# A fused attention and MLP block on one core: the query copy of the last units moved to ScalarE, the gate steps moved to another slot, and the drain reordered

## The chip, the cores and the metric

The kernel runs on one core of a Trainium2 chip. The metric is the device time of one execution in microseconds (us). Three runs of the kernel before gave 1291.65, 1294.03 and 1294.50 us, so the median is 1294.03 us. The engines have the profile's names: PE is TensorE, PEld its weight loads, DVE is VectorE, ACT is ScalarE, POOL is GpSimd and SP is SyncE, which here only issues DMAs.

## What is computed

The reference, cut to what matters (2048 tokens, width 512, 32 heads of 128, 2048 cached keys per head):

```python
xn = layernorm(x)
q  = (xn @ wq) split into 32 heads of 128
p  = softmax(q @ k_cache^T * 128 ** -0.5)
s  = concat over heads (p @ v_cache) @ wo
h  = gelu(layernorm(xn) @ w1), its four column groups shifted by +1, -1, +2, -2 tokens
x1 = xn + h @ w2
g  = silu(x1 + gelu(layernorm(x1) @ w3) @ w4)
out = x + s * g
```

The MLP side ends in g, called the gate here. The kernel carries twice the gate, which explains the factor 0.5 that stands in front of it below.

## The kernel before

**Units and slots.** The attention is cut into 128 units, one for each head and block of 512 queries, in eight groups of four heads; inside a group the four query blocks follow each other, and inside a block the four heads. A unit has eight slots, p = 0 to 7, and each slot handles 256 keys. All engines' instructions are pinned: each engine runs them in the order in which the program issues them. The loop over slots (L656 to L713) is therefore the schedule.

**One slot.** PE multiplies two 128-key blocks by the queries into one of two PSUM tiles `ps_s` (`s_slot`, L178). ACT takes the exponential of the whole 128x1024 tile into `pT` (L188). Five slots later PE multiplies those weights with the values into `ps_o` (`pv_slot`, L207; the lag is `LAG = 5`).

**One unit on DVE.** The eight `pT` quarters are added up to one 128x512 tile: `add_first` at slot 4 (L194), `add_next` at slot 6 (L199), and at slot 0 of the following unit `add_last`, which is a third add and two folds (L199, L204, L205). At slot 3 of the following unit PE sums that tile over its partitions with four 128x1 matmuls against a column of ones (`sums`, L217), DVE takes the reciprocal (L227), SP writes it to DRAM (`dr`, L229) and at slot 4 reads it back broadcast to all partitions (`rb`, L244). At slot 2 of the unit after that, `norm` (L255) multiplies `ps_o` by `rb` into `oT`.

**Queries.** `q_mm` puts the next unit's queries into the PSUM tile `ps_q` with two matmuls in slot 0 and two in slot 1. `q_copy` (L173 to L176) brings them to the bf16 tile `qT` at slot 2; before the change DVE does it (L175). `ps_q` shares a single PSUM buffer (tag "xa") with `ps_wo`.

**Output projection.** When the four heads of a query block are done, its four blocks of 128 tokens get their product with Wo, one in each of the following units: two matmuls at slot 4, two at slot 5 (`wo_mm`, L260), and `wo_post` (L316) at slot 6 adds the result into the f32 sum `s_acc` (L322). In the last group `wo_post` also applies the gate and adds x (L326, L328) and stores the 128 tokens (L329). For query blocks 2 and 3 the projection of the group before the last is deferred: its normalized heads are kept in `oS`, and the last group's projection of these tokens has eight matmuls instead of four. So units 125, 126 and 127 have four more matmuls at slot 4 than others.

**Last units.** `QUIET` is 121 (units count from 0), and the MLP's matmuls are all done by then. `tail_open` loads the gate `gf` and the input `xf` of the last four token blocks. `gate_sum` (L290), called once in each of the units 122 to 125 at slot 7 (L653), turns `s_acc` of one of these token blocks into 0.5 * s_acc * gate + x with two DVE steps (L293, L295), so that only the deferred part remains to be added in the end.

**Drain.** After the loop (L715 to L749) the last unit, 127, still owes PE the value products of slots 3 to 7, all of its denominator sums (`split_sums`, L231, which feeds `ps_sum` with several partly added tiles, four 128x1 matmuls for each), one projection left over for token block 11 (`t11`), and the projection of token blocks 12 to 15, for which two PSUM tiles `pa` and `pb` hold two blocks each. `last_scale` (L297) multiplies by the gate on DVE (L299), `last_out` (L302) adds `s_acc` on POOL for two blocks and on DVE for two (L304), and SP stores them (L305). Slot 6 of unit 127 has a fold of its own on DVE in place of an add (L698). The drain's order of work is written out by hand.

Of the kernel before, what the change touches and what calls it, by code (L numbers as in the profile page):

```python
# [8 lines left out]
ACT = mybir.ActivationFunctionType  # L9
# [8 lines left out]
def kernel(  # L18
# [15 lines left out]
    nc = tc.nc  # L34
# [94 lines left out]
    def at(n, fn):  # L129
        todo[n].append(fn)  # L130
# [41 lines left out]

    def q_copy(u):  # L173
        qT = qtp.tile([P, 512], BF16, name="qT")
        pin(nc.vector.tensor_copy(out=qT[:], in_=st[u].pop("psq")[:]))  # L175
        st[u]["qT"] = qT  # L176

    def s_slot(u, p):  # L178
# [12 lines left out]
    def add_first(u):  # L191
        s = st[u]
        s["acc"] = trp.tile([P, 4, 512], BF16, name="acc")
        pin(nc.vector.tensor_tensor(  # L194
            out=s["acc"][:], in0=s["pT"][0][:], in1=s["pT"][1][:], op=ALU.add))
# [11 lines left out]
    def pv_slot(u, p):  # L207
        g, qt, hh = units[u]
        s = st[u]
        if p == 0:  # L210
            s["o"] = psO.tile([P, 512], FP32, name="ps_o")
        pT = s["pT"][p // 2]
        for j in range(2):
            kc = 2 * p + j
            mm(s["o"][:], vBs[g * HG + hh][:, kc, :], pT[:, 2 * (p % 2) + j, :], kc == 0, kc == KC - 1)
# [15 lines left out]
    def split_sums(u, parts):  # L231
        s = st[u]
        if "ps" not in s:
            s["ps"] = psX.tile([P, 4], FP32, tag="xm", name="ps_sum")
        for a, first, last in parts:
            a = a.rearrange("k (p j) -> k j p", j=4)
            for j in range(4):
                mm(s["ps"][:, j:j + 1], a[:, j, :], ones_t[:], first and j == 0, last and j == 3)
        if parts[-1][2]:
            recip(s, s["ps"])  # L240

    def bcast(u):
        st[u]["rb"] = rp.tile([P, 512], FP32, name="rb")
        pin(nc.sync.dma_start(  # L244
            out=st[u]["rb"][:], in_=st[u]["dr"][:].rearrange("p j -> (p j)").partition_broadcast(P)))

    def norm(u, pieces=1):
        g, qt, hh = units[u]
        s = st.pop(u)
        if hh == 0:  # L250
            oTs[(g, qt)] = otp.tile([P, HG, 512], BF16, name="oT")
        w = 512 // pieces
        for i in range(pieces):
            c = slice(i * w, (i + 1) * w)
            pin(nc.vector.tensor_tensor(  # L255
                out=oTs[(g, qt)][:, hh, c], in0=s["o"][:, c], in1=s["rb"][:, c], op=ALU.mult))
# [3 lines left out]
    def wo_mm(g, t, hhs):  # L260
        if hhs[0] == 0:
            wo_box[0] = psX.tile([P, D], FP32, tag="xa", name="ps_wo")
        held = g == NG - 1 and (NG - 2, t // 4) in deferred
        if held and hhs[0] == 0:
            wo_part(wo_box[0][:], g - 1, t, range(HG), True, False)
        wo_part(wo_box[0][:], g, t, hhs, hhs[0] == 0 and not held, hhs[-1] == HG - 1)

    def wo_part(ps, g, t, hhs, first, last):
        oT = oTs[(g, t // 4)]
        ts = t % 4  # L270
        for hh in hhs:
            mm(ps, oT[:, hh, ts * P:(ts + 1) * P], wos[g * HG + hh][:],
               first and hh == hhs[0], last and hh == hhs[-1])
# [16 lines left out]
    def gate_sum(t):  # L290
        gf, xf = tl[t]
        sa = s_acc[:, t, :]
        pin(nc.vector.scalar_tensor_tensor(  # L293
            out=sa, in0=sa, scalar=0.5, in1=gf[:], op0=ALU.mult, op1=ALU.mult))
        pin(nc.vector.tensor_tensor(out=sa, in0=sa, in1=xf[:], op=ALU.add))  # L295
# [6 lines left out]
    def last_out(t, eng):  # L302
        gf, xf = tl.pop(t)
        pin(eng.tensor_tensor(out=xf[:], in0=gf[:], in1=s_acc[:, t, :], op=ALU.add))  # L304
        pin(nc.sync.dma_start(out=out2d[t * P:(t + 1) * P, :], in_=xf[:]))  # L305
# [10 lines left out]
    def wo_post(g, t):  # L316
        ps = wo_box.pop(0)
        sa = s_acc[:, t, :]
        if g == 0:
            pin(nc.vector.tensor_copy(out=sa, in_=ps[:]))  # L320
            return
        pin(nc.vector.tensor_tensor(out=sa, in0=ps[:], in1=sa, op=ALU.add))  # L322
        if g < NG - 1:
            return
        xl, gl = fin.pop(t)
        pin(nc.vector.scalar_tensor_tensor(  # L326
            out=gl[:], in0=sa, scalar=0.5, in1=gl[:], op0=ALU.mult, op1=ALU.mult))
        pin(nc.vector.tensor_tensor(out=xl[:], in0=gl[:], in1=xl[:], op=ALU.add))  # L328
        pin(nc.sync.dma_start(out=out2d[t * P:(t + 1) * P, :], in_=xl[:]))  # L329
# [320 lines left out]

    at(QUIET * SPU, tail_open)
    for t in range(4 * LQ, NT):
        at((QUIET + 1 + t % 4) * SPU + 7, lambda t=t: gate_sum(t))  # L653

    wo_todo = deque()
    for n in range(NS):  # L656
        u, p = divmod(n, SPU)
        s_slot(u, p)
        m = n - LAG
        if m >= 0:  # L660
            pv_slot(*divmod(m, SPU))
        if u == 0 and p in (0, 2, 4):
            q_mm(1 + p // 2, range(DC))
        if u == 0 and p in (1, 3, 5):
            q_copy(1 + p // 2)
        if p in (0, 1) and HG - 1 <= u < NU - 1:
            q_mm(u + 1, (2 * p, 2 * p + 1))
        if p == 0 and u >= 1:
            add_last(u - 1)
        if p == 2 and HG - 1 <= u < NU - 1:  # L670
            q_copy(u + 1)
        if p == 2 and u >= 2:
            norm(u - 2)
            gg, qq, hh = units[u - 2]
            if hh == HG - 1 and (gg, qq) in deferred:
                pin(nc.sync.dma_start(out=o_d[qq][:], in_=oTs[(gg, qq)][:]))
            elif hh == HG - 1:
                wo_todo.extend((gg, 4 * qq + ts) for ts in range(4))
                if gg == NG - 1:
                    fin_load(4 * qq)  # L680
        if p == 3 and u >= 1:
            sums(u - 1)
        if p == 4 and u >= 1:
            bcast(u - 1)
        if p in (4, 5) and wo_todo:
            wo_mm(*wo_todo[0], (0, 1) if p == 4 else (2, 3))
        if p == 6 and wo_todo:
            gg, t = wo_todo.popleft()
            wo_post(gg, t)
            if gg == NG - 1 and t % 4 < 3:  # L690
                fin_load(t + 1)
        if p == 4:
            add_first(u)
        if p == 6 and u < NU - 1:
            add_next(u, 2)
        if p == 6 and u == NU - 1:
            a = st[u]["acc"]
            pin(nc.vector.tensor_tensor(out=a[:, 0:2, :], in0=a[:, 0:2, :], in1=a[:, 2:4, :], op=ALU.add))  # L698
        if p in (2, 3, 6, 7):
            w = 2 * u + (p >= 4)  # L700
            i = p % 2
            if i == 0:
                want = -(-(w + 1 - W0) * NCH // (W1 - W0)) if w >= W0 else 0
                window.pop("run", None)
                if done < min(want, NCH):
                    if done in hooks:
                        hooks.pop(done)(n)
                    window["run"] = chunks.popleft()
                    done += 1
            if "run" in window:  # L710
                window["run"](i, n)
        for fn in todo.pop(n, ()):
            fn()  # L713
# [4 lines left out]
    gg, t11 = wo_todo.popleft()  # L718
    ts = [4 * LQ + j for j in range(4)]
    norm(U - 1)  # L720
    pv_slot(U, 3)
    wo_mm(gg, t11, (0, 1))
    pv_slot(U, 4)
    wo_mm(gg, t11, (2, 3))
    wo_post(gg, t11)
    pv_slot(U, 5)
    pa = psS.tile([P, 2, 512], FP32, name="ps_s")
    wo_part(pa[:, 0, :], GL - 1, ts[0], range(HG), True, False)
    split_sums(U, [(s["acc"][:, i, :], i == 0, False) for i in range(2)]
               + [(s["pT"][2][:, i, :], False, False) for i in range(4)]  # L730
               + [(s["pT"][3][:, i, :], False, False) for i in range(2)])
    pv_slot(U, 6)
    split_sums(U, [(s["pT"][3][:, i, :], False, i == 3) for i in range(2, 4)])
    bcast(U)
    pv_slot(U, 7)
    wo_part(pa[:, 1, :], GL - 1, ts[1], range(HG), True, False)
    pb = psS.tile([P, 2, 512], FP32, name="ps_s")
    for j in (2, 3):
        wo_part(pb[:, j % 2, :], GL - 1, ts[j], range(HG), True, False)
    dst = [(pa, pa, pb, pb)[j][:, j % 2, :] for j in range(4)]  # L740
    for j in range(4):
        wo_part(dst[j], GL, ts[j], range(HG - 1), False, False)
    norm(U, 2)
    for j in range(4):
        wo_part(dst[j], GL, ts[j], (HG - 1,), False, True)
        last_scale(ts[j], dst[j])
    for j in range(4):
        last_out(ts[j], nc.gpsimd if j < 2 else nc.vector)
    ph.close()  # L749


# [28 lines left out]
```

## Time and profile before

| What | us |
|---|---|
| median of three runs | 1294.03 (1291.65 to 1294.50) |
| profiled execution, its own time | 1291.04 |
| its span, first to last instruction | 1289.3 |
| PE busy | 1257.6 (98%) |
| ACT busy | 1111.7 (86%) |
| DVE busy | 1017.9 (79%) |
| POOL busy | 145.8 (11%) |
| granted TensorE clock, mean | 0.998 |
| unit 121, from its `sums` to the next unit's | 8.76 |
| units 123 and 124, the same | 9.66 each |
| from the end of the loop's matmuls (1269.70) to the end of the span | 19.60 |

The page's busy time of PE counts the modelled length of pipelined matmuls; a 128x512 matmul shows about 0.38 us by itself, while in a dense stretch one starts every 0.216 us. Where the text speaks of PE time it uses these starts. "Start to start" on DVE and ACT means the distance between the starts of two instructions that follow each other without a wait; they overlap a little (a lone exponential takes 1.02 us, three in a run take 2.86 us).

### The profile page before, as it was taken

To read this page: it belongs to the slowest core of one execution; us is meant where nothing else is said; L and a number is where in the kernel's file an instruction comes from. 1 tells how busy PE (TensorE), PEld (TensorE's weight loads), DVE (VectorE), ACT (ScalarE), POOL (GpSimd) and SP (SyncE) were. 2 spreads that over 40 slices of the span, in tenths; PEclk is the share of its full clock that TensorE was granted. 3 is DMA by queue.
4 is the path that set the end of the run, shared out by engine and by line. 5 is a ranking of instruction groups with operands and counts; after the bars stand their busy time and mean duration, and the time that the engine had idled before them with its cause. 6 is when DMAs were issued, how large, how long until landed. Compare 5 with 4: busy or idle time off the path is not lost.

```text
span 1289.3 us, 17150 instructions
## 1 busy us (share of the span) xinstructions
PE 1257.6 (98%) x6148; PEld 577.4 (45%) x6272; DVE 1017.9 (79%) x1396; ACT 1111.7 (86%) x1189; POOL 145.8 (11%) x253
## 2 busy tenths in 40 slices
PE   6999999999999999999999999999999999999997
PEld 3444444444444444444444444444444444444443
DVE  5888888888788877778887778887777888777985
ACT  5899998888999988899988889998888999988873
POOL 4432002333110110000001000000000000000100
PEclk9999999999999999999999999999999999999999
DMA  8635553456533465125563256523445224553422
GB/s 180 152 95 113 85 74 79 102 132 124 106 76 73 99 114 96 37 66 83 98 94 63 50 96 92 91 41 77 92 83 86 49 58 80 86 98 61 145 54 54
DMA packets 224790, 113.89 MB, mean 88 GB/s; under 512 B 192640, under 2 KB 201344, under 8 KB 224704
## 3 DMA queue, kind: packets, MB, share of 16 engines
q1 hardware_dynamic: 213056, 85.51, 36.4%
q0 software_dynamic: 9248, 26.49, 7.9%
q8 instruction: 49, 0.80, 0.3%
q10 hardware_dynamic: 2400, 0.79, 0.3%
q14 instruction: 37, 0.30, 0.1%
HBM read 82.58 MB, written 9.70 MB: 72 GB/s over the span
## 4 chain that ended last, share of the span: by engine, by line
PE 81%; ACT 8%; DVE 6%; DMA 2%; issue 2%; POOL 1%; SPq 0%; DVEq 0%; ACTq 0%; POOLq 0%
PE ps_s L113 29%; PE ps_o L113 28%; PE ps_m L113 9%; PE ps_wo L113 8%; PE ps_q L113 7%; ACT pT L188 6%; DVE acc L199 2%; ACT sq L396 1%; PE ps_sum L113 1%; ACT pre L426 1%; DVE acc L204 1%; DMA rb<-dr 1%; DMA xin<-in_A_x_dram 0%; DVE bn L344 0%; DMA kT<-in_A_k_cache_dram 0%
## 5 line engine op out<-in xcount | busy, mean ns | idle before, releaser
L188 ACT ACTIVATE pT<-ps_s 128x1024 bf16<-128x1024 f32 x1024 | 1012.8, 1030 | 149.6 <-PE ps_s L113 143.3
L113 PE MATMUL ps_s<-qT,kT 128*128 128x512 bf16 x2007 | 601.3, 380 | 4.5 <-ACT pT L188 0.9
L113 PE MATMUL ps_o<-pT,vb 128*128 128x512 bf16 x2007 | 600.4, 379 | 3.4 <-DMA vb<-in_A_v_cache_dram 0.9
L199 DVE TENSOR_TENSOR acc<-acc,pT 128x2048 bf16<-128x2048 bf16 x254 | 309.8, 1220 | 59.7 <-ACT pT L188 54.5
L113 PEld LDWEIGHTS <-vb 128*128 128x128 bf16 x2048 | 199.3, 97 | 243.1 <-DMA vb<-in_A_v_cache_dram 1.4
L113 PEld LDWEIGHTS <-kT 128*128 128x128 bf16 x2048 | 195.8, 98 | 239.6 <-issue 21.4
L194 DVE TENSOR_TENSOR acc<-pT 128x2048 bf16<-128x2048 bf16 x128 | 155.8, 1217 | 28.8 <-ACT pT L188 28.7
L113 PE MATMUL ps_q<-xnT,wq_h 128*128 128x512 bf16 (+1 forms) x512 | 152.1, 381 | 1.7 <-ACT xnT L371 1.1
L113 PE MATMUL ps_wo<-wo_h,oT 128*128 128x512 bf16 x450 | 135.1, 379 | 0.6
L322 DVE TENSOR_TENSOR s_acc<-ps_wo,s_acc 128x512 f32<-128x512 f32 x100 | 69.0, 690 | 83.9 <-PE ps_wo L113 77.7
L255 DVE TENSOR_TENSOR oT<-ps_o,rb 128x512 bf16<-128x512 f32 x129 | 87.3, 677 | 7.3 <-DMA rb<-dr 7.2
L204 DVE TENSOR_TENSOR acc<-acc 128x1024 bf16<-128x1024 bf16 x127 | 87.9, 692 | 4.3
L175 DVE CAST qT<-ps_q 128x512 bf16<-128x512 f32 x127 | 87.1, 686 | 4.4 <-PE ps_q L113 4.4
L113 PEld LDWEIGHTS <-wq_h 128*128 128x128 bf16 x524 | 51.9, 100 | 62.7 <-issue 3.8
L113 PEld LDWEIGHTS <-oT 128*128 128x128 bf16 x480 | 46.8, 98 | 59.7 <-issue 3.7
L113 PE MATMUL ps_m<-xn2T,w_sb 128*128 128x512 bf16 x217 | 65.1, 379 | 0.3
L113 PE MATMUL ps_m<-w_sb,h2T 128*128 128x512 bf16 x219 | 62.9, 379 | 0.3
L545 POOL DMA_DIRECT2D w_sb<-in_B_w_dram x28 | 21.1, 755 | 353.7 <-PE ps_m L113 313.8
L205 DVE TENSOR_TENSOR acc<-acc 128x512 bf16<-128x512 bf16 x127 | 54.0, 425 | 4.3
L113 PEld LDWEIGHTS <-acc 128*128 128x128 bf16 x516 | 37.0, 116 | 37.3 <-DVE acc L205 9.4
L227 DVE RECIPROCAL rc<-ps_sum 128x4 f32<-128x4 f32 x128 | 23.0, 180 | 37.7 <-PE ps_sum L113 36.9
L577 POOL DMA_DIRECT2D g_d<-xr x16 | 8.7, 546 | 343.6 <-DVE xr L575 343.6
(66 smaller groups left out, 592.3 us busy)
## 6 DMA issues: line engine op xcount, KB each, us to landing
rb<-dr SPq DMA_DIRECT2D x128, 256.0 KB, 4.2
vb<-in_A_v_cache_dram SPq DMA_DIRECT2D x64, 256.0 KB, 4.8
w_sb<-in_B_w_dram POOLq DMA_DIRECT2D x28, 256.0 KB, 4.0
wo_h<-in_A_wo_dram SPq DMA_DIRECT2D x32, 128.0 KB, 4.1
wq_h<-in_A_wq_dram SPq DMA_DIRECT2D x28, 128.0 KB, 4.5
kT<-in_A_k_cache_dram SPq DMA_TRANSPOSE x128, 4.9
xn_d<-xn POOLq DMA_DIRECT2D x16, 128.0 KB, 3.4
dr<-rc SPq DMA_DIRECT2D x128, 2.0 KB, 1.5
```

The source lines that it names most:

```text
L113: pin(nc.tensor.matmul(out=out, lhsT=lhsT, rhs=rhs, start=start, stop=stop))
L175: pin(nc.vector.tensor_copy(out=qT[:], in_=st[u].pop("psq")[:]))
L188: pin(nc.scalar.activation(out=s["pT"][-1][:, jj:jj + 2, :], in_=sps[:], func=ACT.Exp, scale=SCALE))
L194: pin(nc.vector.tensor_tensor(out=s["acc"][:], in0=s["pT"][0][:], in1=s["pT"][1][:], op=ALU.add))
L199: pin(nc.vector.tensor_tensor(out=a[:], in0=a[:], in1=st[u]["pT"][i][:], op=ALU.add))
L204: pin(nc.vector.tensor_tensor(out=a[:, 0:2, :], in0=a[:, 0:2, :], in1=a[:, 2:4, :], op=ALU.add))
L205: pin(nc.vector.tensor_tensor(out=a[:, 0, :], in0=a[:, 0, :], in1=a[:, 1, :], op=ALU.add))
L227: pin(nc.vector.reciprocal(out=rc[:], in_=ps[:]))
L255: pin(nc.vector.tensor_tensor(out=oTs[(g, qt)][:, hh, c], in0=s["o"][:, c], in1=s["rb"][:, c], op=ALU.mult))
L322: pin(nc.vector.tensor_tensor(out=sa, in0=ps[:], in1=sa, op=ALU.add))
L396: pin(nc.scalar.activation(out=sq[:], in_=pre[:], func=ACT.Square, scale=GELU_A ** 0.5))
L545: pin(nc.gpsimd.dma_start(out=w[:], in_=w3_v[:, :, fc * P:(fc + 2) * P]))
```

## The change

There are three edits in the loop and one in the drain.

1. `q_copy(u)` for u above 121, which is issued at slot 2 of units 121 to 126, becomes an ACT instruction (Identity).
2. `gate_sum` goes from slot 7 to slot 4 of the same units 122 to 125. It comes behind `add_first` there.
3. In unit 127 the fold on DVE goes from slot 6 to slot 4, behind `add_first`.
4. In the drain the denominator sums stand between the value products of slots 3, 4 and 5, ahead of those of 6 and 7; the leftover projection of token block 11 comes behind all value products; and the projections of token blocks 12 to 15 are grouped so that all of PE's matmuls come ahead of the four scalings.

```diff
     def q_copy(u):
         qT = qtp.tile([P, 512], BF16, name="qT")
-        pin(nc.vector.tensor_copy(out=qT[:], in_=st[u].pop("psq")[:]))
+        if u > QUIET:
+            pin(nc.scalar.activation(out=qT[:], in_=st[u].pop("psq")[:], func=ACT.Identity))
+        else:
+            pin(nc.vector.tensor_copy(out=qT[:], in_=st[u].pop("psq")[:]))
         st[u]["qT"] = qT
...
     for t in range(4 * LQ, NT):
-        at((QUIET + 1 + t % 4) * SPU + 7, lambda t=t: gate_sum(t))
+        at((QUIET + 1 + t % 4) * SPU + 4, lambda t=t: gate_sum(t))
...
         if p == 4:
             add_first(u)
+        if p == 4 and u == NU - 1:
+            a = st[u]["acc"]
+            pin(nc.vector.tensor_tensor(out=a[:, 0:2, :], in0=a[:, 0:2, :], in1=a[:, 2:4, :], op=ALU.add))
         if p == 6 and u < NU - 1:
             add_next(u, 2)
-        if p == 6 and u == NU - 1:
-            a = st[u]["acc"]
-            pin(nc.vector.tensor_tensor(out=a[:, 0:2, :], in0=a[:, 0:2, :], in1=a[:, 2:4, :], op=ALU.add))
...
     norm(U - 1)
+    held = range(HG)
+    ready = range(HG - 1)
     pv_slot(U, 3)
-    wo_mm(gg, t11, (0, 1))
+    split_sums(U, [(s["acc"][:, i, :], i == 0, False) for i in range(2)]
+               + [(s["pT"][2][:, i, :], False, False) for i in range(4)])
     pv_slot(U, 4)
-    wo_mm(gg, t11, (2, 3))
-    wo_post(gg, t11)
+    split_sums(U, [(s["pT"][3][:, i, :], False, False) for i in range(2)])
     pv_slot(U, 5)
-    pa = psS.tile([P, 2, 512], FP32, name="ps_s")
-    wo_part(pa[:, 0, :], GL - 1, ts[0], range(HG), True, False)
-    split_sums(U, [(s["acc"][:, i, :], i == 0, False) for i in range(2)]
-               + [(s["pT"][2][:, i, :], False, False) for i in range(4)]
-               + [(s["pT"][3][:, i, :], False, False) for i in range(2)])
-    pv_slot(U, 6)
     split_sums(U, [(s["pT"][3][:, i, :], False, i == 3) for i in range(2, 4)])
     bcast(U)
+    pv_slot(U, 6)
     pv_slot(U, 7)
-    wo_part(pa[:, 1, :], GL - 1, ts[1], range(HG), True, False)
+    wo_mm(gg, t11, (0, 1, 2, 3))
+    wo_post(gg, t11)
+    pa = psS.tile([P, 2, 512], FP32, name="ps_s")
     pb = psS.tile([P, 2, 512], FP32, name="ps_s")
+    dst = [(pa, pa, pb, pb)[j][:, j % 2, :] for j in range(4)]
+    for j in (0, 1):
+        wo_part(dst[j], GL - 1, ts[j], held, True, False)
+        wo_part(dst[j], GL, ts[j], ready, False, False)
     for j in (2, 3):
-        wo_part(pb[:, j % 2, :], GL - 1, ts[j], range(HG), True, False)
-    dst = [(pa, pa, pb, pb)[j][:, j % 2, :] for j in range(4)]
+        wo_part(dst[j], GL - 1, ts[j], held, True, False)
+    norm(U, 2)
+    for j in (0, 1):
+        wo_part(dst[j], GL, ts[j], (HG - 1,), False, True)
+    for j in (2, 3):
+        wo_part(dst[j], GL, ts[j], range(HG), False, True)
     for j in range(4):
-        wo_part(dst[j], GL, ts[j], range(HG - 1), False, False)
-    norm(U, 2)
-    for j in range(4):
-        wo_part(dst[j], GL, ts[j], (HG - 1,), False, True)
         last_scale(ts[j], dst[j])
-    for j in range(4):
-        last_out(ts[j], nc.gpsimd if j < 2 else nc.vector)
+        if j < 2:
+            last_out(ts[j], nc.gpsimd)
+    for j in (2, 3):
+        last_out(ts[j], nc.vector)
```

## The prediction, made before the change was run

> **What bounds the kernel now.** I read the page's busy table first (PE 98% of the span), then the table by stage cut at the `sums` of the last units, since the whole change lies behind 1205 us, then the chain, and last the timelines of DVE, ACT and PE there. By stage:
>
> ```profile
> 1206.47:1215.23 8.76, 8.71 (x47) 4.05 (x47) 7.76 (x12) 7.75 (x9) 1.07 (x2) 1.00 0.27 76
> 1215.23:1224.70 9.47, 8.71 (x43) 3.77 (x41) 8.54 (x14) 8.47 (x9) 1.61 (x3) 1.00 0.36 86
> 1224.70:1234.36 9.66, 8.95 (x44) 3.97 (x45) 8.89 (x14) 7.86 (x9) 1.08 (x2) 1.00 0.31 68
> ...
> 1244.02:1254.55 10.53, 9.76 (x47) 4.35 (x49) 8.89 (x14) 7.86 (x9) 0.00 (x0) 1.00 0.22 52
> 1254.55:1263.94 9.39, 9.03 (x44) 3.94 (x45) 7.69 (x12) 7.23 (x9) 0.00 (x0) 1.00 0.19 42
> ...
> 1269.70:1289.30 19.60, 12.25 (x88) 5.84 (x87) 7.82 (x14) 0.41 (x1) 2.31 (x2) 0.88 0.21 56
> ```
>
> Columns: length, then busy PE, PEld, DVE, ACT, POOL. Unit 121 is pure PE: 40 large matmuls at 0.216 and the sums make 8.76. The gated units 122 to 125 have the same matmuls (125 four more, 0.86) and last up to 0.9 longer. From 1215.23 to 1263.94 are 48.71; five units at 8.76 and 0.86 make 44.66 (126 has four more too, but at its end the four query matmuls of unit 127 are missing). So **4.05 us of PE are lost**. The chain of unit 123 says to whom:
>
> ```profile
> 1227.17 0.44 PE ps_wo L113 x2
> 1227.62 0.02 issue
> 1227.64 0.70 DVE s_acc L322
> ...
> 1229.44 1.22 DVE acc L199
> 1230.65 0.61 DVE s_acc L293
> 1231.27 0.02 issue
> 1231.29 0.69 DVE s_acc L295
> 1231.98 1.15 DVE acc L199
> ...
> 1234.36 0.29 PE ps_sum L113 x4
> ```
>
> The loop is: sums (S), the Wo matmuls, then DVE's s_acc at S+2.94, and from there to the next sums 6.72. Without the gate this second leg is 5.58 (unit 126: 1258.36 to 1263.94). The query cast is not on it: in each gated unit DVE idles 0.59 to 1.5 ahead of s_acc. The drain's chain:
>
> ```profile
> 1275.07 0.19 DVE rc L227
> 1275.27 0.02 issue
> 1275.29 1.98 DMA dr<-rc
> 1277.26 0.02 issue
> 1277.28 3.46 DMA rb<-dr
> ...
> 1281.31 0.40 PE ps_s L113
> ...
> 1281.73 0.70 DVE gf L299
> 1282.44 0.04 issue
> 1282.48 0.39 PE ps_s L113
> ...
> 1282.89 1.30 DVE gf L299 x2
> ```
>
> PE's 24 filling matmuls end at 1280.67, just as `rb` lands (1280.73). Then PE and DVE alternate: the matmul of block 13 waits for the scaling of block 12, that of 15 for that of 14, as they share a PSUM tile. DVE ends at 1286.54; the last store and the close take 2.76 more.
>
> **Query copy.** It takes six casts off DVE, 0.60 each start to start (1214.67 to 1215.27). ACT gets six: the nearest row is `pre<-ps_m`, same engine, function and shape, 0.595 (x72). Exponentials take 1.02 alone and 0.92 in a run, so 0.10 overlaps and a copy in a run costs 0.50. ACT's waits in unit 121 add up to 1.00 (0.33+0.23+0.27+0.17), so throughput is there. The place is the catch: ACT serves in order, and the copy stands ahead of slot 3's exponential, for which `add_first` waits. In unit 121 the run of three starts at 1205.27, slot 3's ends at 1207.21 = S+0.74 and `add_first` starts at S+0.77. With the copy, S+1.27. For PE, slot 5's scores (1207.89) need the buffer that slot 3's exponential then frees at 1207.71: hidden by 0.18. Without that cover it is at most the copy and one restart, 0.595+0.18 = 0.78 a unit (sums that had to wait take 0.29, others 0.11: a restart is 0.18). The shared PSUM buffer is next wanted at 1207.46 and free at 1206.8. A table load is priced at nothing: the trace has one in all (1.283) although 76 Identity instructions stand among Exp and Tanh.
>
> [...]
>
> **Gate at slot 4.** Net it takes 6.72-5.58 = 1.14 off the second leg and puts it ahead of s_acc: `add_first` to gate 1.13 (as L199 to L293), 0.72, 0.65 (between 0.61 and 0.72), so s_acc can start at A+2.50 if `add_first` starts at A. The next sums follow at A+2.50+5.58 = A+8.08, or when PE is ready: 8.76, or 8.94 after a wait. After a wait X in front of the sums, ACT has caught up: A = 1.27-X, but not below S+0.55, where `add_first` stands in unit 127, which has no cast.
> - Unit 122: A 1.27, 9.35 (before 9.47); X = 0.59.
> - 123: A 0.68, so 8.76, below 8.94: 8.94 (9.66); X = 0.
> - 124: as 122, 9.35 (9.66).
> - 125: Wo sets s_acc at S+3.81, 9.39; PE needs 9.63+0.18 = 9.81 (10.53).
> - 126: no gate; Wo at S+3.63 without a restart, 9.21 (9.39).
>
> Gains 0.12+0.72+0.31+0.72+0.18 = **2.05**. Bounds: the loss of 4.05 all gone on one side, copies that PE pays (-4.68) on the other. `gf` and `xf` were loaded by 1207, the earliest gate is after 1217. s_acc up to 0.9 later still leaves `ps_wo` free at S+4.5, and the query matmuls want it at S+5.3. No DMA moves with the gate.
>
> **Drain.** In before's clock; all of it shifts with the loop. The fold moved to slot 4 sits in DVE's wait of 2.06 ahead of s_acc (1265.7 to 1267.7), takes 0.68, costs nothing, and lets the unit 126 `norm` start 0.68 earlier. PE is at 1269.86 behind slot 3's products. Then 24 sums 0.78 (32 took 1.04), products 0.46 (1274.35 to 1274.81), 8 sums 0.24, 0.46, 0.24: 1272.04, reciprocal at 1272.07, **3.00 earlier**. The exponentials have ended by 1270.11. `dr` is issued at 1272.29, and with 1.98+3.46 `rb` is there at 1277.73; the first half of `norm` is done at 1278.26. On SP, block 11's store is now behind `rb` and not ahead of `dr`; it waits for nothing important, but runs beside `rb`'s end, so `rb` may take the median 4.2. PE meanwhile: 4 products, 8 Wo for block 11, 14 and 8: 34 at 0.216 and a switch of 0.1, 1279.48. So `norm` is covered by 1.2 us. Ten more, 1281.64. The scalings of 12 and 13 fit before that (`pa` ready at 1279.91), and POOL's adds (1.15 each) run to 1283.0. Scalings of 14, 15 and two adds: 0.60+0.60+1.28 from 1281.66, 1284.15 against 1286.54: **2.39** gained. PE does no less; what is late next is PE itself. Bounds: `rb` at the longest landings seen (4.6+6.2) would come at 1283.1, ten matmuls and the tail then end at 1288.3, a loss of 1.8; at the shortest (1.4+3.2) nothing more is gained.
>
> **Sum.** 2.05+2.39 = 4.44. The profiled execution's 1291.04 becomes 1286.6. It lies 3.0 below the median of the runs shown; on the median, 1294.03-4.44 = **1289.6**, -0.34%. A measurement here tells about 0.2%, 2.6 us, from no change.
>
> **Rivals.**
> 1. **A new wait replaces the old.** Copy and gate together push s_acc as late as the gate did: a latch, sums to wait for, cast time on neither path. For: A+2.50 is S+3.77 in units without a wait, beyond Wo's 2.75. Against: a wait lets ACT catch up. Then only the drain gains: 1291.6. 22%.
> 2. **All 4.05 go**, if slot 3's exponential is less late than I hold: 4.05+2.39, 1287.6. Against: ACT is strictly in order. 13%.
> 3. **ScalarE becomes the bound: slower.** If slot 3's exponential frees its buffer over 0.18 later than I have it, PE waits for scores in all six units, 6x0.78 = 4.68, with the gates' loss kept: +4.68-2.39 = +2.3, 1296.3; a table load in each unit would add 1.28 apiece, 1304. For: the 0.18 is thin. Against: in units with a wait ACT is early. 6%.
> 4. **The drain doesn't deliver**, `rb` or a PSUM tile's release comes late: the loop alone, 1292.0, at the longest landings 1293.8. 8%.
>
> **The numbers.** Forecast 51%. Forecast and rival 2 are faster by over 0.2%: 0.64; rivals 1 and 4 within: 0.30; rival 3 slower: 0.06. The range goes from 1286.5 (my sum on the profiled time; rival 2 lies inside) to 1292.6 (rival 1 and most of 4): rival 3 and the rest of 4, some one in ten, are out, and as much for the spread of runs.
>
> **What would show it.** Sums to sums of units 122 to 126 as listed, alternating between long and short, with the gate between L194 and L322; `add_first` about 0.5 later after the sums where these did not wait; an Identity of about 0.6 at slot 2 of ACT and one table load in all; no PE wait for ACT ahead of scores; reciprocal 3 us earlier against the loop's end; PE without a gap from 1269.7 on until its end; four scalings, the last two back to back behind PE's last matmul. I am wrong if the units stay at 9.66, if PE waits on `pT`, or if a gap ahead of the last ten matmuls shows `rb` uncovered.

## The result, and the profile after

| | before | changed |
|---|---|---|
| first comparison, median (4 runs each) | 1293.85 (1291.65 to 1294.50) | 1287.40 (1286.52 to 1288.11) |
| its ratio | | 0.9953, interval 0.9936 to 0.9970 |
| second comparison, median (26 and 5 runs) | 1291.54 (1290.14 to 1295.34) | 1286.49 (1286.22 to 1286.88) |
| its ratio | | 0.9959, interval 0.9947 to 0.9971 |
| profiled execution, time and span | 1291.04, 1289.3 | 1287.13, 1285.4 |
| sums of unit 121 to sums of unit 127, by the chain ("loop stretch") | 57.47 | 55.36 |
| from there to the end of the span ("drain stretch") | 25.36 | 22.89 |

The change makes the kernel 0.4 to 0.5% faster. The forecast of -0.34% (ratio 0.9966) lies in both intervals, and the measured 1287.40 lies in the range of 1286.5 to 1292.6, near its lower end. The two stretches that the edits touch got 2.11 and 2.47 us shorter, together 4.58, where 2.05 and 2.39 were forecast. The rest of the difference between the medians is not in these two stretches and is dealt with below.

The stage table of the changed kernel, cut at the sums as that of before (length, then busy PE, PEld, DVE, ACT and POOL, granted clock, DMA):

```profile
1207.15:1215.93 8.78, 8.73 (x48) 4.06 (x47) 7.30 (x11) 8.14 (x10) 1.61 (x3) 1.00 0.26 76
1215.93:1225.24 9.31, 8.73 (x43) 3.77 (x42) 8.07 (x13) 8.67 (x11) 1.08 (x2) 1.00 0.31 83
1225.24:1234.18 8.94, 8.94 (x49) 4.13 (x50) 8.56 (x13) 7.82 (x9) 1.07 (x2) 1.00 0.31 74
1234.18:1243.50 9.32, 8.74 (x45) 3.81 (x43) 8.25 (x13) 8.68 (x11) 1.07 (x2) 1.00 0.21 67
1243.50:1253.31 9.81, 9.76 (x52) 4.63 (x54) 8.91 (x13) 7.82 (x9) 0.00 (x0) 1.00 0.16 50
1253.31:1262.51 9.20, 8.84 (x44) 3.76 (x42) 6.88 (x11) 8.32 (x10) 0.00 (x0) 1.00 0.20 43
```

Units 122 to 126 last 9.31, 8.94, 9.32, 9.81 and 9.20, against a forecast of 9.35, 8.94, 9.35, 9.81 and 9.21. Long and short units alternate, since a unit whose sums had to wait gives ACT the time to catch up for the next one. The chain of a long one, unit 122, names the new wait:

```profile
1214.73 0.83 ACT pT L191
1215.56 0.09 issue
1215.65 0.59 ACT qT L176
1216.24 0.93 ACT pT L191
1217.17 0.02 issue
1217.19 0.04 DVE acc L197
1217.23 1.10 issue
1218.34 0.69 DVE s_acc L296
...
1219.66 0.69 DVE s_acc L325
```

The query copy (L176) stands between two exponentials, the first add (L197) starts behind the second of them at S+1.26, if S = 1215.93 is the start of the sums, then the gate (L296), and only then s_acc (L325) at S+3.73, where the Wo product alone would let it start at S+2.75. So rival 1 of the prediction, a new wait in place of the old, is half true: it happens in units 122 and 124, as the forecast had it, and not in 123.

The chain of the drain:

```profile
1268.43 0.77 PE ps_sum L113 x24
1269.20 0.45 PE ps_o L113 x2
1269.65 0.25 PE ps_sum L113 x8
1269.90 0.45 PE ps_o L113 x2
1270.35 0.24 PE ps_sum L113 x8
...
1271.48 1.73 PE ps_wo L113 x8
1273.20 6.92 PE ps_s L113 x32
1280.12 0.02 issue
1280.15 1.29 DVE gf L302 x2
1281.44 0.60 DVE xf L307
```

No DMA is in it any more: it is PE from the first sums to its last matmul, and two scalings and two adds behind it. The reciprocal comes 8.12 us after the sums of unit 127 (1270.63 and 1262.51), before it was 11.13 (1275.07 and 1263.94). The timeline there has the last `norm`, released by the DMA, and the ten matmuls that need it:

```profile
1276.43 0.76 DVE L258 TENSOR_TENSOR oT<-ps_o,rb 128x256 bf16<-128x256 f32 x2 [1.32 <-DMA rb<-dr]
...
1277.79 2.32 PE L113 MATMUL ps_s<-wo_h,oT 128*128 128x512 bf16 x10
```

PE does not wait for `norm`: `rb` lands 1.4 before the ten matmuls start.

### The profile page after: what moved, and what is told of

Read it like the earlier page. It is cut to its first block, busy times and chain, and to the rows that moved or that the text cites. A ratio compares the mean times of both kernels' runs of the same rounds, so it can differ in the third digit from the quotient of the medians.

```text
span 1285.4 us, 17152 instructions
## 1 busy us (share of the span) xinstructions
PE 1256.3 (98%) x6148; PEld 578.2 (45%) x6272; DVE 1015.0 (79%) x1390; ACT 1114.1 (87%) x1195; POOL 145.0 (11%) x253
## 4 chain that ended last, share of the span: by engine, by line
PE 82%; ACT 9%; DVE 5%; issue 2%; DMA 1%; POOL 1%; SPq 0%; DVEq 0%; ACTq 0%; POOLq 0%
PE ps_s L113 30%; PE ps_o L113 28%; PE ps_m L113 9%; PE ps_wo L113 7%; PE ps_q L113 7%; ACT pT L191 6%; DVE acc L202 2%; ACT sq L399 1%; PE ps_sum L113 1%; ACT pre L429 1%; DVE acc L207 1%; DMA xin<-in_A_x_dram 0%; DMA kT<-in_A_k_cache_dram 0%; ACT sq L408 0%; DMA rb<-dr 0%
## 5 line engine op out<-in xcount | busy, mean ns | idle before, releaser
L197 DVE TENSOR_TENSOR acc<-pT 128x2048 bf16<-128x2048 bf16 x128 | 155.8, 1217 | 32.4 <-ACT pT L191 32.1
L325 DVE TENSOR_TENSOR s_acc<-ps_wo,s_acc 128x512 f32<-128x512 f32 x100 | 68.9, 689 | 80.3 <-PE ps_wo L113 74.8
L178 DVE CAST qT<-ps_q 128x512 bf16<-128x512 f32 x121 | 82.9, 685 | 3.9 <-PE ps_q L113 3.9
```

Source lines behind the costliest of these rows:

```text
L197: pin(nc.vector.tensor_tensor(out=s["acc"][:], in0=s["pT"][0][:], in1=s["pT"][1][:], op=ALU.add))
```

## The experiments

Each kernel was profiled once and timed beside the kernel before. The stretches come from the profile, by the chain's starts of the sums of units 121 and 127. Times are medians; the interval is that of the ratio.

| kernel | loop stretch | drain stretch | time | before beside it | interval |
|---|---|---|---|---|---|
| before | 57.47 | 25.36 | | | |
| e0, before again | 57.46 | 24.97 | 1291.44 | 1291.54 | 0.9990 to 1.0007 |
| changed | 55.36 | 22.89 | 1287.40 | 1293.85 | 0.9936 to 0.9970 |
| e9, changed again | 55.36 | 22.83 | 1286.49 | 1291.54 | 0.9947 to 0.9971 |
| e1, loop only | 55.37 | 26.31 | 1289.01 | 1291.38 | 0.9974 to 0.9993 |
| e2, drain only | 57.47 | 22.83 | 1288.36 | 1291.38 | 0.9966 to 0.9985 |
| e3, gate moved, cast on DVE | 54.91 | 22.82 | 1286.04 | 1291.38 | 0.9943 to 0.9973 |
| e4, copy on ACT, gate late | 57.50 | 22.82 | 1288.59 | 1291.38 | 0.9971 to 0.9990 |
| e6, sums early, alternating | 55.35 | 24.53 | 1288.37 | 1291.54 | 0.9961 to 0.9980 |
| e7, sums late, grouped | 55.36 | 25.05 | 1288.74 | 1291.54 | 0.9965 to 0.9983 |
| e8, fold late | 55.36 | 23.46 | 1287.31 | 1291.32 | 0.9955 to 0.9980 |
| e5, gate on POOL | 58.83 | 22.91 | 1292.38 | 1291.32 | 0.9998 to 1.0016 |
| e10, gate steps spread | 53.86 | 22.78 | 1284.73 | 1291.32 | 0.9937 to 0.9961 |
| e11, the same with the copy on ACT | 54.05 | 22.80 | 1285.83 | 1291.32 | 0.9942 to 0.9969 |

**Repeats (e0, e9).** Both programs unchanged.

> The kernel before, unchanged, once more. It asks how far executions of one program differ, and where. My theory: the part ahead of unit 121 differs by some us between executions, while the loop stretch (57.47) and the drain stretch (25.36) repeat within 0.1. Rival: the last stretches differ as much, and then the differences read from single profiles are worth little.

> The changed kernel, unchanged, once more, timed on the same chip as the kernel before. My theory: loop stretch 55.36 and drain stretch 22.89 within 0.1, and faster than before by 4.4 to 4.6 us, as these two stretches say, within the scatter. Rival, a gain elsewhere: 6 us or more again.

The loop stretch repeats to 0.01. The drain stretch of the changed kernel repeats to 0.06, that of before does not: 25.36 and 24.97. The part ahead moves too: the sums of unit 121 start between 1204.99 and 1208.02 in the profiles of all kernels but e5, though their code up to there is almost the same; in the two pairs of one program they differ by 0.80 and 0.24. So single profiles are good for the loop stretch and the changed drain, less so for before's drain and whole spans. The median gap of the repeat is 5.05 us, the stretches of these two profiles say 4.24 and those of the first pair 4.58, and the interval goes from 3.7 to 6.8 us. With 25.55 for before's drain (the mean of before, e0 and e1), the medians of e1 to e4 and e6 to e10 give a gain within 0.3 of what their two stretches say (e1 with the same 25.55), that of e11 0.7 less: nothing points to a gain elsewhere. The first comparison's 6.45 rests on four runs of before with a median 2.3 above that of the 26.

**Halves (e1, e2).** e1 is the kernel before with the edits below; e2 is the changed kernel with the same edits undone, so that the fold and the drain are left.

```diff
-        pin(nc.vector.tensor_copy(out=qT[:], in_=st[u].pop("psq")[:]))
+        if u > QUIET:
+            pin(nc.scalar.activation(out=qT[:], in_=st[u].pop("psq")[:], func=ACT.Identity))
+        else:
+            pin(nc.vector.tensor_copy(out=qT[:], in_=st[u].pop("psq")[:]))
...
-        at((QUIET + 1 + t % 4) * SPU + 7, lambda t=t: gate_sum(t))
+        at((QUIET + 1 + t % 4) * SPU + 4, lambda t=t: gate_sum(t))
```

> Query copy on ScalarE and gate at slot 4, the drain as before. Two stretches are read: from the sums of unit 121 to those of unit 127 (before 57.47 us, changed kernel 55.36), and from there to the end of the span (25.36 and 22.89). My theory: the loop's gain and the drain's are separate and add up, so 55.4 and 25.4, some 2.1 us faster than before. Rival, a gain elsewhere: the medians lie 6.4 apart while the two profiled executions lie 3.9 apart, so something ahead of unit 121 got faster through the program's change; then this kernel or the drain alone is faster by over 2 us more than its two stretches say.

> The fold and the drain as changed; cast on VectorE and gate at slot 7 as before. My theory: loop stretch 57.5, drain stretch 22.9, some 2.4 to 2.5 us faster than before. Rival, the drain lives on the loop's gain (its transfers meet others when the loop is late): drain stretch 24 or more. Rival, a gain elsewhere: faster by over 4.5.

The loop's and the drain's edits work each by itself: 55.37 beside 55.36, 22.83 beside 22.89. In time they gave 2.37 and 3.02 us, together 5.4, beside 5.05 for both at once. What did not fit is the drain stretch of e1: 26.31, not 25.4. Its chain shows why (start, duration):

```profile
1274.74 2.00 DMA dr<-rc
1276.74 0.02 issue
1276.75 4.21 DMA rb<-dr
1280.96 0.03 issue
...
1281.05 0.44 DVE oT L258
1281.49 0.05 issue
1281.54 0.40 PE ps_s L113
```

The broadcast took 4.21 here, 3.46 in the profile of before, 3.04 in e0. With late denominators the broadcast is on the path: the drain stretch is 26.31, 25.36 and 24.97 in this order. Why the broadcast itself takes 3.04 to 4.21 was not studied. In the eight profiles that have the changed drain it is 22.78 to 22.91. The early denominators took not only the mean of that round trip off the path but its scatter.

**Which edit earns the loop's gain (e3, e4).** Both have the changed drain. e3, against the changed kernel:

```diff
-        if u > QUIET:
-            pin(nc.scalar.activation(out=qT[:], in_=st[u].pop("psq")[:], func=ACT.Identity))
-        else:
-            pin(nc.vector.tensor_copy(out=qT[:], in_=st[u].pop("psq")[:]))
+        pin(nc.vector.tensor_copy(out=qT[:], in_=st[u].pop("psq")[:]))
```

e4, against the changed kernel:

```diff
-        at((QUIET + 1 + t % 4) * SPU + 4, lambda t=t: gate_sum(t))
+        at((QUIET + 1 + t % 4) * SPU + 7, lambda t=t: gate_sum(t))
```

> As the changed kernel, but the query cast stays on VectorE: of the loop's edits only the gate at slot 4. My theory: the cast costs VectorE 0.60 ahead of add_first after a wait, the copy on ScalarE delays add_first by 0.50 without a wait, so neither is better: units 122 to 126 take 8.85, 9.23, 9.23, 9.81, 9.21, loop stretch 55.1, about 0.3 shorter than in the changed kernel. Rival, freeing VectorE of six casts is a good part of the gain: loop stretch over 56.

> As the changed kernel, but the gate stays at slot 7: of the loop's edits only the copy on ScalarE. My theory: the cast is not on the loop from Wo to s_acc to the next sums, so nothing is gained: loop stretch 57.4 to 57.5, drain stretch 22.9. Rival, VectorE's total work sets the gated units: six casts of 0.60 less, four of them in gated units, loop stretch 55.1 to 56.

e4 stays at 57.50: the copy alone earns nothing, though it takes six casts of 0.6 off DVE. e3 has 54.91: without the copy the loop is 0.45 shorter than with it. The PE timeline of e3 at the sums of units 124 and 125, with the wait ahead of them:

```profile
1233.61 0.29 PE L113 MATMUL ps_sum<-ones_t,acc 128*128 128x1 bf16 x4 [0.21 <-DVE acc L205]
...
1242.77 0.29 PE L113 MATMUL ps_sum<-ones_t,acc 128*128 128x1 bf16 x4 [0.22 <-DVE acc L205]
```

and that of the changed kernel at those of units 123 and 125:

```profile
1225.24 0.29 PE L113 MATMUL ps_sum<-ones_t,acc 128*128 128x1 bf16 x4 [0.53 <-DVE acc L208]
...
1243.50 0.29 PE L113 MATMUL ps_sum<-ones_t,acc 128*128 128x1 bf16 x4 [0.53 <-DVE acc L208]
```

With the cast on DVE the sums wait 0.2 behind units 123 and 124, with the copy on ACT 0.5 behind units 122 and 124. The units of e3 take 8.76, 8.82, 9.16, 9.16, 9.81 and 9.20 (121 to 126). So almost all of the 0.45 is unit 122, 8.82 beside 9.31; units 123 and 124 together take 18.32 with the cast and 18.26 with the copy. In e3 DVE runs through units 122 to 124 without a wait, and the chain follows it there, through the cast: with the gate at slot 4, DVE's own work has become the bound of 123 and 124, and the cast lies on the path. The whole gain of the loop is the gate's. The Trainium skill, "ScalarE: Activation LUTs", Rules for kernel authors, gives relu, max, min, add and mul to VectorE for its rate; it does not name a copy. Here the rate is no reason against ACT (0.59 a copy, 0.68 a cast on DVE); what costs is the copy's place in ACT's queue.

**The drain in parts (e6, e7, e8).** All three have the changed loop. e6, against the changed kernel:

```diff
+    for j in (2, 3):
+        wo_part(dst[j], GL, ts[j], ready, False, False)
     norm(U, 2)
-    for j in (0, 1):
-        wo_part(dst[j], GL, ts[j], (HG - 1,), False, True)
-    for j in (2, 3):
-        wo_part(dst[j], GL, ts[j], range(HG), False, True)
     for j in range(4):
+        wo_part(dst[j], GL, ts[j], (HG - 1,), False, True)
         last_scale(ts[j], dst[j])
```

e7 has the sums, the fillers and the last `norm` in the order of the kernel before, and differs from it in the drain by this:

```diff
     for j in range(4):
         wo_part(dst[j], GL, ts[j], (HG - 1,), False, True)
-        last_scale(ts[j], dst[j])
     for j in range(4):
-        last_out(ts[j], nc.gpsimd if j < 2 else nc.vector)
+        last_scale(ts[j], dst[j])
+        if j < 2:
+            last_out(ts[j], nc.gpsimd)
+    for j in (2, 3):
+        last_out(ts[j], nc.vector)
```

e8, against the changed kernel, with the fold itself unchanged:

```diff
-        if p == 4 and u == NU - 1:
+        if p == 6 and u == NU - 1:
```

> As the changed kernel, but the last Wo matmul of each token block stands directly ahead of its scaling, as in the kernel before: of the drain's edits only the early denominators. My theory: TensorE gets through its filling work without the wait of 0.64 for the normalized head, and then alternates with VectorE as before: drain stretch 24.8 (25.36 less 0.53). Rival, the late denominators were the whole of the drain's loss: 23.

> As the changed kernel, but denominators and fillers in the drain in the order of the kernel before, only the last four Wo matmuls ahead of the four scalings. My theory: the broadcast reciprocals still land 16.8 after the sums of unit 127, the four matmuls then need 0.86 and the scalings follow each other at 0.60: drain stretch 24.45 (25.36 less 0.91). The two parts alone give 0.53 and 0.91 and together 2.47, since each uncovers what the other hides. Rival, the two add up: one of them gives over 1.4 alone.

> As the changed kernel, but the fold of unit 127 stays at slot 6, behind the three steps of block 10. My theory: VectorE then ends the fold 5.9 after the sums of unit 127 plus 0.4 to 0.5, and TensorE, which wants the folded tile 5.76 after them, waits 0.5 to 0.6 and restarts for 0.1 to 0.2; TensorE is the bound of the drain, so the drain stretch goes from 22.85 to 23.4 to 23.6. Rival, the drain has cover to spare: 22.9.

e6 gains 0.83 instead of 0.53: its first scaling starts 16.97 after the sums, 17.79 before, so the wait of 0.64 and the restart of 0.18 behind it are both gone. e7 gains 0.31 instead of 0.91. Its broadcast landed 16.87 after the sums, 16.79 in the profile of before, so the two can be compared. Its first scaling starts 18.09 after the sums (the forecast of 24.45 had it at 18.01); the other 0.52 that is missing is in the two adds of DVE:

```profile
1278.44 2.49 DVE L302 SCALAR_TENSOR_TENSOR gf<-ps_s,gf 128x512 bf16<-128x512 f32 x4 [0.37 <-PE ps_s L113]
1280.85 1.80 DVE L307 TENSOR_TENSOR xf<-gf,s_acc 128x512 bf16<-128x512 bf16 x2
```

They take 1.80 and not 1.28 as in the other drains; POOL adds beside them from 1279.22 to 1281.49. That neither part alone comes near the 2.47 of both holds: 0.83 and 0.31. e8 loses 0.57 (23.46, forecast 23.4 to 23.6). PE waits for the fold:

```profile
1268.08 0.42 PE L113 MATMUL ps_sum<-ones_t,acc 128*128 128x1 bf16 x8 [0.42 <-DVE acc L701]
```

So the changed drain has no slack in PE, and the small third edit is needed for the fourth.

**The gate on POOL (e5).** Three instructions on POOL replace DVE's two in `gate_sum`; the cast is on DVE, the drain is the changed one.

```diff
+        pin(nc.gpsimd.tensor_tensor(out=sa, in0=sa, in1=gf[:], op=ALU.mult))
+        pin(nc.gpsimd.tensor_scalar(out=sa, in0=sa, scalar1=0.5, scalar2=None, op0=ALU.mult))
+        pin(nc.gpsimd.tensor_tensor(out=sa, in0=sa, in1=xf[:], op=ALU.add))
```

> As the changed kernel, with the cast on VectorE and the gate steps on the idle GpSimd engine, in three instructions (multiply by the gate, by 0.5, add x). Theory one: VectorE is free of the gate, units 121 to 124 take 8.76, 125 9.63, 126 9.21: loop stretch 53.9 against 55.36 in the changed kernel. Theory two: GpSimd's adds hold VectorE's. In the run with late denominators and grouped matmuls a VectorE add that began beside a GpSimd add of 1.15 took 0.5 more. Then three GpSimd steps of at least 1.15 a unit hold VectorE's adds, the sums wait again and the loop stretch is 55 to 57.

Theory two holds, and worse than it said. Little on POOL ties it to the slots, so it ran the gates early, one behind the other, from before 1200 to 1222; its loop stretch of 58.83 does not even contain the first of the waits (1.62 ahead of the sums of unit 121). The timeline of DVE and POOL shows the hold:

```profile
1218.19 1.16 POOL L293 TENSOR_TENSOR s_acc<-s_acc,gf 128x512 f32<-128x512 f32 x1
...
1218.22 1.70 DVE L204 TENSOR_TENSOR acc<-acc 128x1024 bf16<-128x1024 bf16 x1
...
1220.72 0.29 PE L113 MATMUL ps_sum<-ones_t,acc 128*128 128x1 bf16 x4 [2.92 <-DVE acc L205]
```

The fold L204 takes 0.69 elsewhere and 1.70 beside POOL's multiplication of 1.16 that began 0.03 earlier: 1.0 more. The sums waited 2.92, and then PE ran at half its clock (the column after POOL's is the granted clock):

```profile
1222.00:1223.00 1.00, 1.00 (x4) 0.34 (x3) 1.00 (x1) 0.95 (x1) 0.50 (x1) 0.50 0.08 2
1223.00:1224.00 1.00, 1.00 (x4) 0.42 (x3) 0.58 (x1) 0.00 (x0) 0.00 (x0) 0.50 0.00 0
1224.00:1225.00 1.00, 1.00 (x6) 0.40 (x4) 0.00 (x0) 0.53 (x1) 0.00 (x0) 0.86 0.00 0
```

That unit took 10.62 instead of 8.76, without any wait of its own ahead of the sums that end it.

**The gate steps spread over six units (e10, e11).** The cast is on DVE in e10, the copy on ACT in e11; both have the changed drain and spread the eight gate steps:

```diff
-        at((QUIET + 1 + t % 4) * SPU + 4, lambda t=t: gate_sum(t))
+    for u, j, steps in ((0, 0, (0,)), (1, 0, (1,)), (2, 1, (0,)), (3, 1, (1,)), (4, 2, (0, 1)), (5, 3, (0, 1))):
+        at((QUIET + u) * SPU + 4, lambda t=4 * LQ + j, steps=steps: gate_sum(t, steps))
```

> As the changed kernel, with the cast on VectorE; the eight gate steps are spread, all at slot 4: one step each in units 121 to 124, two each in 125 and 126, whose four additional Wo matmuls keep VectorE waiting for 1.1 to 1.5. My theory: one step fits into the wait of 0.76 ahead of s_acc (0.77+1.13+0.72 = 2.62 after the sums, Wo is done at 2.75), so units 121 to 124 take 8.76, 125 9.63, 126 9.21: loop stretch 53.9, 1.5 shorter than in the changed kernel and 3.6 shorter than before; drain stretch 22.85; some 6 us faster than before in all. Rival, VectorE has no true room and any step there costs its time: loop stretch 55 or more.

> As the run with the spread gate steps, but with the query copy on ScalarE as in the changed kernel. My theory: add_first then starts 1.27 after the sums, s_acc at 1.27+1.13+0.72 = 3.12, the next sums could start at 8.70, just inside TensorE's 8.76: loop stretch 53.9 to 54.3, no gain from the copy at all. Rival, the copy frees VectorE: shorter than the run without it by 0.3 or more.

The stage table of e10, units 121, 125 and 126:

```profile
1206.66:1215.42 8.76, 8.76 (x50) 4.06 (x47) 8.37 (x13) 7.76 (x9) 1.61 (x3) 1.00 0.33 76
...
1241.70:1251.32 9.62, 9.62 (x52) 4.45 (x51) 9.05 (x14) 7.75 (x9) 0.00 (x0) 1.00 0.20 46
1251.32:1260.52 9.20, 8.89 (x44) 3.74 (x42) 8.63 (x14) 7.83 (x9) 0.00 (x0) 1.00 0.18 43
```

PE has no gap until unit 126, whose last leg from Wo remains. e10 is 6.6 us faster than before (1284.73 beside 1291.32). Its two stretches are 1.6 shorter than those of the changed kernel (76.64 and 78.25); the two were not timed in the same comparison. e11 is 0.19 longer in the loop: with the gate out of the way the copy still earns nothing.

## Why the prediction was right, point by point

- **The loop without the cast on it.** Right for the kernel before: e4 took the cast off and gained nothing.
- **Gate at slot 4.** Right in size and in the alternation, unit by unit within 0.04 (2.11, forecast 2.05); of the 1.50 that the loop still takes above e10's 53.86, putting the cast back on DVE wins 0.45 (e3), and cutting the gate to the size of the waits the rest.
- **The cover of the copy.** Too good by 0.16: I put the scores of slot 5 at the chain's 1207.89, where the timeline of before starts them at 1207.73, just 0.02 behind the release of 1207.71 that I had worked out for the buffer with the copy. The changed kernel shows it: its scores start at 1208.43, S+1.28 instead of S+1.26, and unit 121 takes 8.78 instead of 8.76, as it does in e4 and e11. Rival 3 was nearer than its 6% were meant to say, but its price of 0.78 a unit did not come; unit 121 lost 0.02 and no restart. The copies took 0.59 each, and the trace still has one table load.
- **Early denominators.** 3.01 earlier, forecast 3.00. The first half of the last `norm` was ready at 1276.86 and PE wanted it at 1277.79: a cover of 0.9, forecast 1.2. I named block 11's store beside `rb` as a danger; `rb` took 3.4 there, and nothing waited for it.
- **End of the drain.** DVE ends 20.12 after the sums of unit 127 (22.60 before): 2.48, forecast 2.39. My bounds for `rb` were wider than needed upward, but I had not seen that before's own drain moves with it: 24.97 to 26.31 in three profiles. The step "1284.15 against 1286.54" took one sample of a moving quantity. Over the three, the drain's gain is 25.55-22.85 = 2.7; that 2.47 came so near 2.39 is in part luck, as e0 alone would have made it 2.1 and e1 3.5.
- **From the profile to the median.** I moved the sum of 4.44 to the median of three runs. That gave 1289.6, which is 2.2 above the measured 1287.40. From the 1291.54 of the 26 later runs of before, the sum gives 1287.10, where the second comparison measured 1286.49. So the sum was right to within its scatter and the base was high: the start of the stretches moves by 3 us over the profiles. What moves it was not studied.

## What to carry to other kernels

Find the loop that closes on the waiting instruction and move what lies on it; work taken off a busy engine beside that loop (six casts here) is worth nothing, and where it lands in another engine's queue ahead of something awaited it can cost. Look again after the move, as the loop may then close elsewhere. Small steps can be hidden where the engine waits anyway, if they are cut to the size of each wait. In a drain, start the longest round trip first, fill behind it, and group what two engines would otherwise alternate on; alone, the two parts gave together less than half of what both gave at once.

## What the runs showed of the hardware that was not expected

- **DVE is held beside POOL on such operations.** A bf16 fold of DVE took 1.70 instead of 0.69 beside a POOL multiplication of 1.16, an add pair 1.80 instead of 1.28 beside a POOL add. The Trainium skill, "SBUF — State Buffer", Who interferes with whom, says so: a DVE instruction with two SBUF inputs contends with a GpSimd instruction that reads SBUF, over a shared pair of ports that the page calls an exclusive lock. The rows agree: the fold was 1.0 longer where POOL had 1.1 still to run. The scalings, which read one tile from PSUM and one from SBUF, kept their 0.60 start to start beside the same POOL adds (four in 2.49 in e7).
- **A halved clock after a wait of 2.92 us, seen once (e5).** TensorE's granted clock was 0.50 for some 3 us behind it. The skill's "TensorE: Matmul & The Clock Gate", Part 1, gives a window of about 3.4 us of idleness; here PE had been without a matmul for 2.92 and without a weight load for 3.41, so this case does not tell whether a shorter wait would do. The wait of 1.62 in the same run left the next sums' unit at a clock of 1.00.
